# Group norm on one core: replacing a five-engine schedule by looped engine programs with GpSimd left idle

## The chip, the cores and the metric

The kernel runs on one core of a Trainium2 chip. The profile lists the core's work by engine: TensorE (PE; PEld is its weight load), VectorE (DVE), ScalarE (ACT), GpSimd (POOL) and SyncE (SP), which here only issues transfers. It counts 16 DMA engines, which in the kernel before read 134.22 MB from HBM and wrote 134.22 MB to it; SBUF is the memory on the chip that holds the tiles. The metric is device time in microseconds (us).

## The reference, cut to what matters

```python
B, C, H, W, G = 128, 1024, 32, 16, 32          # bfloat16
xr = x.reshape(B, G, C // G, H, W)
mu = xr.mean(axis=(2, 3, 4), keepdims=True)
var = ((xr - mu) ** 2).mean(axis=(2, 3, 4), keepdims=True)
xn = (xr - mu) / jnp.sqrt(var + 1e-5)
return xn.reshape(x.shape) * g[None, :, None, None] + b[None, :, None, None]
```

Each of the 4096 (image, group) pairs has 32 channels of 512 numbers. A tile is 128 pairs, one per partition, of 16,384 bf16 numbers: 4 MB. There are 32 tiles. Each must come in once (134 MB in all) and go out once (134 MB).

## The kernel before

Six tile buffers. Loads and stores share SyncE's queue. TensorE sums a tile (32 matmuls with an identity matrix, 512 columns each, into one 128x512 tile in PSUM, the memory that this kernel's matmuls write to), VectorE reduces the 512 sums to the mean, ScalarE squares and sums the tile in two halves and takes the square root, and three engines share the scaling of the 32 channels: 13 on GpSimd, 16 on VectorE, 3 on ScalarE.

```python
XBUFS = 6; UPFRONT = 6; RUN = 3; FIRST_RUN = 2; QUARTERS = 4
STORE_IN_PARTS = 2; ACT_SHARE = 2; LAST_SHARE = 3; POOL_SHARE = 13

def shifted(i):                      # these two tiles are loaded in quarters
    return i == 0 or i == NT - RUN

def A(i):                            # scale tile i
    if not in_parts(i):
        for n in range(POOL_SHARE):
            scale_on("pool", i, KC - LAST_SHARE - POOL_SHARE + n)
        for k in range(KC - LAST_SHARE - POOL_SHARE):
            scale_on("dve", i, k)
        ...
        return
    for c in range(NQ):              # the last two tiles: in quarters, stored as they are done
        for k in range(c * KQ, (c + 1) * KQ):
            on_act = i == NT - 1 and k >= (c + 1) * KQ - ACT_SHARE
            scale_on("act" if on_act else "dve", i, k)
        S(i, c, c + 1)

def finish(i):                       # called between ScalarE's two halves of tile i+1
    for k in range(KC - LAST_SHARE, KC):
        scale_on("act", i, k)
    S(i, 0, NQ)                      # store
    if i % RUN == FIRST_RUN - 1:     # after each third store: three loads
        ... L(j)
```

Everything is unrolled: 3885 instructions are recorded.

## Time and profile before

| | before |
|---|---|
| time, median of the first 3 runs (4 with the change beside it) | 632.48 us (632.44) |
| span of the profiled run | 630.9 us |
| busy: DMA / ACT / DVE / POOL / PE | 90% or more in 38 of 40 slices / 85% / 60% / 55% / 41% |
| DMA rate, 60 to 540 us | 429 to 434 GB/s |

First the page of the kernel before: span, busy time per engine, then rows of 40 slices of the span (a digit is the busy share in tenths), then the instruction fetches (queue, packets, MB, share), then three groups of instructions (line, engine, operation, output<-input, shapes, count; busy us, mean ns; idle time before them and what ended it).

```profile
span 630.9 us, 3885 instructions
PE 257.5 (41%) x1005; PEld 106.1 (17%) x1025; DVE 378.9 (60%) x645; ACT 537.6 (85%) x268; POOL 345.2 (55%) x523
...
DVE  0087766665665666277616774664766177777650
ACT  4599999998997699489949995996899499999950
POOL 0077776665664666177716664663776166777000
...
DMA  8999999999999999999999999999999999999996
...
q8 instruction: 8, 0.13, 0.1%
q14 instruction: 15, 0.12, 0.0%
...
L245 ACT ACTIVATE ja<-xt,negmean 128x8192 fp8e5<-128x8192 bf16 x60 | 426.5, 7109 | 51.5 <-DVE jd L190 51.4
...
L369 DVE TENSOR_SCALAR xt<-xt,scl,bia 128x512 bf16<-128x512 bf16 x536 | 351.3, 729 | 39.8 <-POOL bia L354 39.8
L369 POOL TENSOR_SCALAR xt<-xt,scl,bia 128x512 bf16<-128x512 bf16 x390 | 307.4, 801 | 3.4 <-POOL bia L354 0.3
```

Read it as follows. No compute engine fills its row; the DMA row is full from the second slice to the last but one. A scaling takes VectorE 729 ns while GpSimd also scales.

Next, stretches of the same kernel: busy us of each engine, granted clock, DMA share, GB/s.

```profile
300.00:360.00 60.00, 23.44 (x94) 9.76 (x96) 35.55 (x57) 51.45 (x25) 34.30 (x51) 0.70 1.00 432
...
600.00:620.00 20.00, 0.00 (x0) 0.00 (x0) 8.75 (x28) 8.73 (x11) 0.00 (x0) 0.50 0.98 415
620.00:631.00 11.00, 0.00 (x0) 0.00 (x0) 0.00 (x0) 0.00 (x0) 0.00 (x0) 0.50 0.53 226
```

In mid-run the DMA share is 1.00. At the end no engine computes; DMA alone runs, and more and more of its 16 engines fall idle (share 0.53 from 620 us on).

### The profile page before, as it was taken

The page shows a single profiled execution, that of the slowest core. Times are in us where ns is not written, and L with a number is a line of the kernel's source. Part 1 is how long each engine was busy: PE and PEld are TensorE (multiplying, and loading weights), DVE is VectorE, ACT ScalarE, POOL GpSimd, SP SyncE. Part 2 cuts the span into 40 slices and gives each one's busy share as a digit, 9 for nine tenths or more (in the row PEclk, how much of TensorE's full clock was granted, in tenths as well). Part 3 has the DMA queues.
Part 4 walks back from the last instruction along what each step waited for, and adds up shares of the span by engine and source line. Part 5 has one row for each costly group of instructions (what it writes and reads, how often), then busy time and mean ns, then how long its engine had stood idle before and what let it go on. Part 6 is the DMA issues. An engine that isn't in the chain of part 4 may idle for free.

```text
span 630.9 us, 3885 instructions
## 1 busy us (share of the span) xinstructions
PE 257.5 (41%) x1005; PEld 106.1 (17%) x1025; DVE 378.9 (60%) x645; ACT 537.6 (85%) x268; POOL 345.2 (55%) x523
## 2 busy tenths in 40 slices
PE   5567509009602750572086018404820770456000
PEld 2223203003201320230032003101300230112000
DVE  0087766665665666277616774664766177777650
ACT  4599999998997699489949995996899499999950
POOL 0077776665664666177716664663776166777000
PEclk9789858658855985587579559855965796679555
DMA  8999999999999999999999999999999999999996
GB/s 366 432 431 428 433 432 425 434 434 432 427 433 433 430 432 432 431 422 433 431 434 430 431 434 432 430 434 438 424 434 432 439 432 430 423 433 429 434 421 290
DMA packets 11063, 268.70 MB, mean 426 GB/s; under 512 B 1312, under 2 KB 1312, under 8 KB 1312
## 3 DMA queue, kind: packets, MB, share of 16 engines
q1 hardware_dynamic: 10944, 268.44, 99.1%
q8 instruction: 8, 0.13, 0.1%
q14 instruction: 15, 0.12, 0.0%
q10 hardware_dynamic: 96, 0.00, 0.0%
HBM read 134.22 MB, written 134.22 MB: 426 GB/s over the span
## 4 chain that ended last, share of the span: by engine, by line
DMA 66%; DVE 10%; ACT 9%; PE 8%; issue 3%; POOL 1%; SPq 1%; DVEq 0%; POOLq 0%; ACTq 0%
DMA out_dram<-xt 41%; DMA xt<-in_x_dram 25%; DVE xt L369 9%; PE pa L167 8%; ACT ja L245 8%; ACT xt L364 1%; SPq L105 0%; POOL scl L338 0%; POOL shift L344 0%; POOL bia L354 0%; ACT rstd L309 0%; DVE jd L190 0%; DVE rstd L313 0%; SPq L382 0%; DVEq L457 0%
## 5 line engine op out<-in xcount | busy, mean ns | idle before, releaser
L245 ACT ACTIVATE ja<-xt,negmean 128x8192 fp8e5<-128x8192 bf16 x60 | 426.5, 7109 | 51.5 <-DVE jd L190 51.4
L167 PE MATMUL pa<-xt,eye 128*128 128x512 bf16 x957 | 246.4, 418 | 320.1 <-DMA xt<-in_x_dram 317.5
L369 DVE TENSOR_SCALAR xt<-xt,scl,bia 128x512 bf16<-128x512 bf16 x536 | 351.3, 729 | 39.8 <-POOL bia L354 39.8
L369 POOL TENSOR_SCALAR xt<-xt,scl,bia 128x512 bf16<-128x512 bf16 x390 | 307.4, 801 | 3.4 <-POOL bia L354 0.3
L167 PEld LDWEIGHTS <-eye 128*128 128x128 bf16 x1024 | 106.0, 106 | 471.1 <-DMA xt<-in_x_dram 319.2
L338 POOL TENSOR_SCALAR scl<-gb,rstd 128x32 f32<-128x32 f32 x31 | 11.1, 359 | 216.2 <-DVE rstd L313 216.2
L190 DVE TENSOR_SCALAR_CACHE_REDUCE jd<-pa 128x512 bf16<-128x512 f32 x32 | 21.8, 682 | 103.0 <-PE pa L167 103.0
L364 ACT ACTIVATE xt<-xt,bia,scl 128x512 bf16<-128x512 bf16 x98 | 72.0, 799 | 0.8 <-DVE bia L325 0.8
L313 DVE RECIPROCAL rstd<-rstd 128x1 f32<-128x1 f32 x32 | 5.2, 163 | 83.8 <-ACT rstd L309 83.8
L245 ACT ACTIVATE ja<-xt,q 128x4096 fp8e5<-128x4096 bf16 x8 | 29.6, 3704 | 6.9 <-DVE jd L190 6.8
L344 POOL TENSOR_SCALAR shift<-scl,negmean 128x32 f32<-128x32 f32 x31 | 11.1, 357 | 3.1
L167 PE MATMUL pb<-xt,eye 128*128 128x512 bf16 x47 | 11.4, 389 | 0.5 <-DMA xt<-in_x_dram 0.4
L245 ACT ACTIVATION_READ_ACCUMULATOR ja<-xt,negmean 128x1 f32 x60 | 11.2, 187 | 0.0
L309 ACT ACTIVATE rstd<-s,v 128x1 f32<-128x1 f32 x30 | 8.8, 294 | 2.8
L274 POOL TENSOR_SCALAR v<-s 128x1 f32<-128x1 f32 x30 | 5.9, 197 | 8.2 <-ACT ja L245 5.8
L217 POOL TENSOR_SCALAR off<-negmean,q 128x1 f32<-128x1 f32 x2 | 0.6, 308 | 16.0 <-DVE jd L190 16.0
L354 POOL TENSOR_TENSOR bia<-shift,gb 128x32 f32<-128x32 f32 x31 | 7.8, 251 | 2.6
L309 ACT ACTIVATE rstd<-var,eps_t 128x1 f32<-128x1 f32 x2 | 0.6, 296 | 8.3 <-DVE jv L293 8.3
L160 DVE COPY gb<-gb_p 128x64 f32<-128x64 f32 x1 | 0.2, 224 | 5.2 <-PE gb_p L152 5.2
L120 ACT ACT_TABLE_LOAD x1 | 1.3, 1283 | 1.7 <-PEq L446 1.7
L190 DVE DVE_READ_ACCUMULATOR jd<-pa 128x1 f32 x32 | 2.5, 79 | 0.0
L245 ACT ACTIVATION_READ_ACCUMULATOR ja<-xt,q 128x1 f32 x8 | 1.5, 186 | 0.0
(18 smaller groups left out, 5.0 us busy)
## 6 DMA issues: line engine op xcount, KB each, us to landing
xt<-in_x_dram SPq DMA_DIRECT2D x30, 4096.0 KB, 29.0
out_dram<-xt SPq DMA_DIRECT2D x30, 4096.0 KB, 36.8
xt<-in_x_dram SPq DMA_DIRECT2D x8, 1024.0 KB, 16.5
out_dram<-xt SPq DMA_DIRECT2D x8, 1024.0 KB, 19.0
gb_b<-in_g_dram ACTq DMA_DIRECT2D x1, 2.0 KB, 3.2
gb_b<-in_b_dram ACTq DMA_DIRECT2D x1, 2.0 KB, 5.3
```

What stands on the lines that cost most here:

```text
L120: chain("act", nc.scalar.activation(out=warm[:], in_=eps_t[:], func=ACT.Sqrt))
L167: nc.tensor.matmul(out=ps[:], lhsT=eye[:], rhs=st["xt"][:, k * MMN : (k + 1) * MMN], start=(k == lo), stop=(k == hi - 1),),
L190: nc.vector.tensor_scalar(out=jd[:], in0=ps[:], scalar1=-inv_n, scalar2=seed, op0=ALU.mult, op1=ALU.add, accum_out=total[:],),
L245: nc.scalar.activation(out=ja[:, 0:w], in_=st["xt"][:, k * w : (k + 1) * w], func=ACT.Square, bias=bias, scale=scale, accum_out=sq, satura ...
L274: nc.gpsimd.tensor_scalar(out=v0[:], in0=s0[:], scalar1=inv_n, scalar2=EPS, op0=ALU.mult, op1=ALU.add,),
L309: nc.scalar.activation(out=rstd[:], in_=last_sum[:], func=ACT.Sqrt, bias=bias[:], scale=scale),
L313: chain("dve", nc.vector.reciprocal(out=rstd[:], in_=rstd[:]))
L338: nc.gpsimd.tensor_scalar(out=scl[:], in0=gam, scalar1=rstd[:], scalar2=None, op0=ALU.mult),
L344: nc.gpsimd.tensor_scalar(out=shift[:], in0=scl[:], scalar1=st["negmean"][:], scalar2=None, op0=ALU.mult,),
L354: nc.gpsimd.tensor_tensor(out=bia[:], in0=shift[:], in1=bet, op=ALU.add),
L364: inst = nc.scalar.activation(out=span, in_=span, func=ACT.Identity, bias=bia, scale=scl)
L369: inst = eng.tensor_scalar(out=span, in0=span, scalar1=scl, scalar2=bia, op0=ALU.mult, op1=ALU.add,)
```

## The change

Intent: give each engine its own program with fixed addresses, looped over the six ring slots, so that few instructions are needed; take GpSimd out; let TensorE sum 12 of the 32 chunks of 512 columns while VectorE adds the other 20 in pairs in one instruction; move the mean to ScalarE. Loads and stores keep their order, but no tile is split any more. The diff cut to its core:

```diff
-    for i in range(NT):
-        Q(i)                       # squares on ScalarE (and the previous tile's last 3 scalings)
-        if i + 1 < NT:
-            M(i + 1); R0(i + 1)    # 32 chunks on TensorE, mean on VectorE
-        V(i); A(i)                 # scale/bias on GpSimd, scaling on GpSimd and VectorE
+    def in_rounds(e, one):         # on TensorE, ScalarE, VectorE, each for itself
+        with nc.Fori(0, TRIPS, 1, engines=[e.engine]) as t:       # TRIPS = 5
+            for c in range(SLOTS):                                # SLOTS = 6
+                one(c, t + 1)
+        for c in range(NT - LOOPED):                              # the last two tiles
+            one(c, TRIPS + 1)
```
```diff
+    # VectorE
+    def one(c, turn):
+        follows = not isinstance(turn, int)
+        then = (c + 1) % SLOTS, turn + (c + 1) // SLOTS
+        if follows:
+            pair(*then)            # the next tile's 20 chunks: 5,120 + 5,120 elements, summed
+        e.wait_ge(stded[c], turn)
+        ...                        # reciprocal, scl, bia: 32 elements each
+        for k in range(KC):        # all 32 scalings of this tile
+            ...
+        ts.then_inc(done[c], 1)
```

(Cut: ScalarE's mean from PSUM, its two squares and two small activations; TensorE's 12 matmuls per tile, 32 for the last; SyncE's list of loads and stores; allocations and semaphores.)

## The prediction

Two passages are cut below, and marked, because no trace or run had shown them: a ceiling for the DMA rate (the trace's stretches show 429 to 434 GB/s), and the item on loop turns, a guess. ("Its packet records" are those of the trace of the kernel before.) The sum came to 632.3 us. It is not written out; what stands of it is the kernel before (632.44 us), 0.7 off for the quarters, 0 to 2 on for the tail, and under 1 either way for fetches. The term for loop turns was put behind the DMA limit and shows, as far as can be read, only in "12 to 15 us per loop turn": 6 x (19.4 - 17) and 6 x (19.4 - 16.5) are 14.4 and 17.4, 2.4 more each.

Four of its numbers do not name all they come from, but the trace of the kernel before gives it. Pairing: a 128x512 sum takes VectorE 0.682 us and a 128x1 reciprocal 0.163; with that as the fixed part, 10 x (0.682 - 0.163) + 0.163 = 5.4. ScalarE's mean: three 128x512 scalings in a row take 2.11 us, 0.70 each, and reading a sum 0.19, together 0.9. Fetches: 8 of 16 KB at 1.01 us and 15 of 8 KB at 0.31 make 13 us. Issue to data: the first load was issued at 0.79 us, its first packet started at 1.82.

> **What bounds the kernel now.** The DMA engines. The row of slices shows DMA busy 90% or more in 38 of 40 slices; stretches of 60 us show a share of 1.00 to 1.01 and 429 to 434 GB/s from 60 to 540 us. ACT is busy 85%, DVE 60%, POOL 55%, PE 41%. The DMA-issuing queue waits long (362 us for VectorE's scaling, 211 for stores), but transfers are always outstanding, so that costs nothing. [...] Its packet records: a 32 KB row takes 1.213 us, an 8 KB piece 0.309. 64 tile transfers are 8 rows each per DMA engine: 64 x 8 x 1.213 = 621 us. The span is 630.9: about 2 us of start, 3 of late packets, and a tail in which the 16 engines finish between 624 and 629.5. Only these 10 us can be won.
>
> **What the change does.**
> - Bytes stay. Tiles 0 and 29 are no longer loaded, 30 and 31 no longer stored, in quarters: 4 x 8 x (4 x 0.309 - 1.213) = -0.7 us per DMA engine.
> - Instruction fetch (0.25 MB, 13 us of one DMA engine, 0.8 if spread) may shrink or be repeated each turn: under 1 us.
> - VectorE: with GpSimd idle, a 128x512 scaling keeps the pace of the trace's last tiles (13 in 4.29 us: 0.33 us), not 0.73. Per tile 32 x 0.33 = 10.5; pairing 5,120 elements, an estimate, 5.4 (from 0.68 for 512, fixed part taken off); small ones with waits 0.9: 17 us.
> - ScalarE: two squares 14.5, mean about 0.9, two small ones 0.6, waits 0.4: 16.5 us; it scales no more.
> - TensorE: 12 x 0.42 = 5 us instead of 13.
> - [...]
>
> A tile in and out costs DMA 19.4 us, so 17 and 16.5 leave over 2 us each: 12 to 15 us per loop turn. Nearly all of the compute change is off the critical path.
>
> **The tail.** Today the last load lands at 571 us; six stores of 9.7 us follow. In the new kernel ScalarE starts tile 29 at about 557 and ends tile 31 near 606, VectorE scales it by 618, and only then its whole store is issued; the slowest DMA engine needs it at about 619, and data starts about 1 us after issue. So the quarters' 0.7 us is about given back: 0 to 2 us lost here.
>
> **Predicted: 632.3 us, range 630.2 to 636.0.** Faster by over 2%: 0.01; within 2%: 0.95; slower by over 2%: 0.04.
>
> **What would show it.** DMA share 1.00 from 60 to 600 us; row packets of 1.213 us; DVE busy near 530 us, scaling at 0.33 to 0.41 us each; ACT near 510; POOL near 0; the last store issued near 618; the chain of waits mostly DMA, ending in one 9.7 us store.
>
> **What would make it wrong.** A VectorE period above 19.4 us (pairing far slower, or many us per branch) would pace the whole loop: several per cent slower. A pace of 15 to 16 us would remove the tail loss: 630.5. Pairing the next tile before scaling this one ties a store to the next load; if that empties the DMA queue at a change of phase, slices under 90% would show it.

## The result, and the profile after

| | before | after |
|---|---|---|
| median (4 runs each) | 632.44 us | 633.04 us |
| lowest to highest | 632.23 to 633.02 | 632.46 to 633.53 |
| ratio of fast runs | | 1.0008 (95%: 0.999 to 1.0025) |

A ratio is the mean time of one kernel's fast runs over that of the other's of the same rounds, so it is not quite the ratio of the medians. The two kernels are the same within 2%, and no difference is resolved. Almost everything inside changed. The same lines of the page, after:

```profile
span 630.3 us, 2508 instructions
PE 157.6 (25%) x405; PEld 52.0 (8%) x405; DVE 522.3 (83%) x1185; ACT 504.0 (80%) x258; POOL 0.8 (0%) x6
...
DVE  1579999999996998599589949994997799499671
ACT  0799999999996999399859958993999399769930
POOL 0000000000000000000000000000000000000000
...
DMA  8999999999999999999999999999999999999996
...
q8 instruction: 1, 0.02, 0.0%
q14 instruction: 3, 0.02, 0.0%
...
L203 ACT ACTIVATE ja<-ring,nm 128x8192 fp8e5<-128x8192 bf16 x64 | 455.9, 7123 | 2.1
L268 DVE TENSOR_SCALAR ring<-ring,scl,bia 128x512 bf16<-128x512 bf16 x1024 | 333.7, 408 | 1.2
...
L236 DVE SCALAR_TENSOR_TENSOR jp<-ring 128x5120 fp8e5<-128x5120 bf16 x31 | 170.1, 5488 | 63.8 <-DMA ring<-in_x_dram 63.8
```

VectorE scales nearly twice as many spans (1024 instead of 536) in less busy time (333.7 instead of 351.3 us), because one takes 408 ns instead of 729. Pairing adds 170 us to it. The DMA row is the same, digit for digit. Instruction fetches fell from 23 packets to 4.

The same stretches, after:

```profile
300.00:360.00 60.00, 13.95 (x36) 4.60 (x36) 51.23 (x117) 48.93 (x25) 0.00 (x0) 0.59 1.01 434
...
600.00:620.00 20.00, 0.00 (x0) 0.00 (x0) 11.69 (x37) 5.04 (x4) 0.00 (x0) 0.50 0.89 383
```

In mid-run DMA moves what it moved before. In the tail its share falls from 0.98 to 0.89: there is a hole. Here is VectorE's order of time after the change, where it is not waiting for a load (start, us, engine, line, operation, count):

```profile
264.36 0.20 DVE L253 RECIPROCAL rstd<-std 128x1 f32<-128x1 f32 x1
...
265.16 10.43 DVE L268 TENSOR_SCALAR ring<-ring,scl,bia 128x512 bf16<-128x512 bf16 x32
275.50 5.49 DVE L236 SCALAR_TENSOR_TENSOR jp<-ring 128x5120 fp8e5<-128x5120 bf16 x1
280.91 0.15 DVE L236 DVE_READ_ACCUMULATOR jp<-ring 128x1 f32 x1
280.91 0.21 DVE L253 RECIPROCAL rstd<-std 128x1 f32<-128x1 f32 x1
```

From one reciprocal to the next are 280.91 - 264.36 = 16.55 us: VectorE's period per tile. Loading and storing a tile costs every DMA engine 16 rows of 32 KB at 1.213 us each, 19.4 us. So VectorE has 2.9 us of slack per tile, or about 17 us per loop turn of six, as long as it waits for nothing else.

### Who ends the program

The traces record 16 landings (semaphore increments) for every transfer: 1,248 for the 78 transfers before, 1,056 for the 66 after. That is as many as the page counts DMA engines, and they are read here as one per DMA engine. The last two stores, for tiles 30 and 31, are informative. All tables of landings below are from those records, in us:

```
                     store 30 lands on       last store    last landing   last landing minus
                   fastest median slowest      issued                    slowest of store 30
before              614.3   616.0   620.1      611.8 *        629.9            9.8
after               613.9   614.2   619.4      616.4          629.1            9.7
                                               (* last quarter of it)
```

A whole store takes one DMA engine 8 x 1.213 = 9.7 us. In both kernels the program ends 9.7 us after the slowest DMA engine finished store 30. After the change, eleven of the sixteen are done by 614.8 and idle until store 31 is issued: that is the hole. But the slowest works until 619.4, when store 31 has already been issued (its first packets start at 617.2). This gives a theory and its rivals:

- **Theory A.** The slowest of the 16 DMA engines ends the program, before and after. Compute is off its path, except where the last store is issued later than that engine needs it. The hole costs nothing.
- **Rival B.** The hole, 2.5 us per DMA engine on average from 612 to 618 us, is lost time: the change gained that much and gave it back in the tail.
- **Rival C.** VectorE's added work, or the loops, cost time that cancels a gain elsewhere.

### The profile page after: what moved, and what is told of

Its sections match the earlier page's. It is cut to its first block, busy times and chain, and to the rows that moved or that the text cites. A ratio compares the mean times of both kernels' runs of the same rounds, so it can differ in the third digit from the quotient of the medians.

```text
span 630.3 us, 2508 instructions
## 1 busy us (share of the span) xinstructions
PE 157.6 (25%) x405; PEld 52.0 (8%) x405; DVE 522.3 (83%) x1185; ACT 504.0 (80%) x258; POOL 0.8 (0%) x6
## 4 chain that ended last, share of the span: by engine, by line
DMA 63%; DVE 26%; ACT 7%; issue 0%; SPq 0%; DVEq 0%
DMA out_dram<-ring 43%; DMA ring<-in_x_dram 20%; DVE ring L268 16%; DVE jp L236 9%; ACT ja L203 7%; DVE bia L259 0%; DVE scl L255 0%; ACT jm L195 0%; SPq L123 0%; ACT var L213 0%; DVE rstd L253 0%; ACT std L217 0%; DVEq L275 0%; SPq L309 0%; SPq L278 0%
## 5 line engine op out<-in xcount | busy, mean ns | idle before, releaser
L203 ACT ACTIVATE ja<-ring,nm 128x8192 fp8e5<-128x8192 bf16 x64 | 455.9, 7123 | 2.1
L268 DVE TENSOR_SCALAR ring<-ring,scl,bia 128x512 bf16<-128x512 bf16 x1024 | 333.7, 408 | 1.2
L173 PE MATMUL ps<-ring,eye 128*128 128x512 bf16 x404 | 157.4, 571 | 411.8 <-DMA ring<-in_x_dram 411.8
L236 DVE SCALAR_TENSOR_TENSOR jp<-ring 128x5120 fp8e5<-128x5120 bf16 x31 | 170.1, 5488 | 63.8 <-DMA ring<-in_x_dram 63.8
L195 ACT ACTIVATE jm<-ps 128x513 fp8e5<-128x513 f32 (+1 forms) x32 | 19.2, 601 | 95.0 <-DVE jp L236 95.0
L173 PEld LDWEIGHTS ps<-ring,eye 128*128 128x128 bf16 x404 | 51.9, 134 | 516.9 <-issue 467.2
L203 ACT ACTIVATION_READ_ACCUMULATOR ja<-ring,nm 128x1 f32 x64 | 12.0, 187 | 0.0
L217 ACT ACTIVATE std<-sq,var 128x1 f32<-128x1 f32 x32 | 9.4, 295 | 1.0
L213 ACT ACTIVATE var<-sq,eps_t 128x1 f32<-128x1 f32 x32 | 9.4, 295 | 1.0
L259 DVE SCALAR_TENSOR_TENSOR bia<-scl,nm,gb 128x32 f32<-128x32 f32 x32 | 8.0, 251 | 1.1
```

The costliest lines, as they stand in the source:

```text
L173: mm = e.matmul(out=sums(c), lhsT=eye[:], rhs=slot(c)[:, k * MM_FREE : (k + 1) * MM_FREE], start=(k == 0), stop=(k == chunks - 1),)
L195: e.activation(out=jm[:, 0 : src.shape[1]], in_=src, func=ACT.Identity, scale=-inv_n, accum_out=nm[:, c : c + 1], saturate=False,).then_in ...
L203: e.activation(out=ja[:], in_=slot(c)[:, h * (F // 2) : (h + 1) * (F // 2)], func=ACT.Square, bias=nm[:, c : c + 1], scale=1.0, accum_out= ...
L213: e.activation(out=var[:], in_=sq[:, 0:1], func=ACT.Identity, bias=eps_t[:], scale=inv_n).then_inc(varred[c], 1)
L217: e.activation(out=std[:, c : c + 1], in_=sq[:, 1:2], func=ACT.Sqrt, bias=var[:], scale=inv_n).then_inc(stded[c], 1)
L236: e.scalar_tensor_tensor(out=jp[:], in0=slot(c)[:, first : first + w], scalar=1.0, in1=slot(c)[:, first + w : first + 2 * w], op0=ALU.mult ...
```

## The experiments

Twelve kernels ran, each beside the kernel before on the same chip. Except for the two with half the stores, all results were correct. The new kernel's ratio to compare with is 1.0008. It was not run again beside them: they ran on three chips, on which the kernel before had medians of 632.83, 632.76 and 632.62 us, against 632.44 beside the new kernel. A ratio is known to about 0.0015, so the difference of two ratios to about 0.002, or 1.4 us: where a run is said below to lie less than that above or below the new kernel, the times alone do not show it, and the traces have to.

### 1. Closing the hole

```diff
-            e.wait_ge(done[i % SLOTS], i // SLOTS + 1)
-            e.dma_start(out=o_v[i], in_=slot(i))...
+            parts = 4 if i == NT - 1 else 1
+            for q in range(parts):
+                e.wait_ge(done[i % SLOTS], i // SLOTS + 1 + q)
+                e.dma_start(<quarter q of tile i>)...
```

> The new kernel with its last tile stored in four parts, each as soon as its eight scalings are done (first part issued near 608.6 us instead of 616.4). Theory A, the slowest of the 16 DMA engines ends the program and was not waiting in the tail (its share of store 30 landed at 619.4 us, data for store 31 flowed from 617.2): the hole of 613 to 617 us in the DMA row closes, but the time stays, within 0.7 us of the new kernel: 0.999 to 1.002 of before. Rival B, the hole of 2.5 us per engine is lost time: 2 to 2.5 us faster than the new kernel, 0.997 of before or less.

Measured: 633.53 us, ratio 1.0011 (0.9997 to 1.0024). DMA's row of 40 slices between 600 and 632 us, first of the new kernel, then of this one:

```profile
DMA  9899899899899799431219299199199191000000
```

```profile
DMA  9979899799799499498997998999954211000000
```

The hole in the first row ("431219", about 612 to 617 us) is gone in the second, where the DMA engines run out one after the other ("954211"). The last landing is at 630.4 us instead of 629.1. That is lag from before the edit matters: store 26 already landed on the slowest DMA engine at 581.9 us instead of 580.7, and store 29 at 610.9 instead of 609.7. From there to the end are two stores in both, 19.5 and 19.4 us. So the hole was free. Rival B falls.

### 2. Making the hole deeper

```diff
+            if is_last(c, turn):
+                for _ in range(2):
+                    waste(1850)          # a useless VectorE instruction of about 2 us, and a drain
             for k in range(KC):          # the last tile's scaling
```

> The new kernel with about 4.2 us of useless VectorE work before the last tile's scaling, so the last store is issued near 620.6 us. Theory A (slowest DMA engine, free at 619.4 us in the new kernel): it waits about 2 us, time up 1.5 to 2.7 us, about 1.004 of before. Rival B (all of the hole counts): up 4.2 us, 1.007 to 1.008.

Measured: 635.35 us, ratio 1.0035 (1.0021 to 1.0049), 2.3 us above the new kernel's median, not the 4.2 of rival B. The last store was issued at 621.6 us, 5.2 us later than in the new kernel's profile (this run was 0.9 us behind already at 569); store 30 landed on the slowest DMA engine at 620.5. So it waited about 2 us: issue plus the 0.85 us to the first packet gives 622.5.

### 3. Taking the pairing out

```diff
-PE_CHUNKS = 12
+PE_CHUNKS = 32                         # and no pair() on VectorE
```

> The new kernel without pairing: TensorE sums all 32 chunks of every tile, VectorE loses 170 us of work. Theory A (compute off the path except in the tail): DMA share 1.00 until 600 us as before; tile 29's mean comes about 4 us later (32 chunks in 9.4 us against pairing in 5.5), ScalarE paces the last three tiles, last store near 620.5 us, time up 1.5 to 4 us: 1.003 to 1.007 of before. Rival C (VectorE's load costs time): faster than the new kernel by over 2 us.

Measured: 633.96 us, ratio 1.002 (1.0005 to 1.0035), about 0.9 us above the new kernel: below the 1.5 to 4 us expected of A, not resolved from it, and no gain, as C would have it. The last store was issued at 619.2 us, 2.8 us later than in the new kernel, not 4; with 0.85 us to the first packet that is just when the slowest DMA engine became free (620.2). VectorE lost 170 us of work, and the time did not fall. What pairing buys is not throughput: it shortens the chain from the landing of tile 29 to the last store: ScalarE starts the squares of tile 29 at 557.71 us with pairing and at 561.35 without.

### 4. How much VectorE work is free

```diff
             ts.then_inc(done[c], 1)
+            if follows and c < 4:
+                waste(1800)              # about 2 us; the second run: twice waste(2560), about 6 us
```

> The new kernel with about 2 us of useless VectorE work after four of the six tiles of each loop turn: 8 us a turn, 40 us in all. Theory A (VectorE has about 17 us of slack per turn: 6 x (19.43 - 16.55)): VectorE busy rises by about 38 us, the time stays within 0.7 us of the new kernel (0.999 to 1.003 of before). Rival C (VectorE's work is paid): up to 40 us slower, 1.06.

> The same with about 24 us a turn, more than the slack of 17. Theory A: VectorE now paces from the first turn on; first scaling at 35.7 us, 31 tiles of 16.55, 5 turns of 24, one scaling and one store: 675 to 695 us. If the slack were larger than 24 us a turn: 633.

Measured: with 8 us a turn 634.58 us, ratio 1.0028 (1.0012 to 1.0045). VectorE's busy time rose by 40 us (562.4 instead of 522.3), the time by about 1.5 us: within the ratio expected of A, but not within 0.7 us of the new kernel. The profile shows where: DMA was idle for about 1.5 us between 117 and 123 us (two slices of 2.5 us busy to 6 and 5 tenths only), in the first loop turn, when compute has not yet gathered a lead. Up to 200 us there is no other such gap, and store 30 landed at 617.7 us in the median instead of 614.2. With 24 us a turn 687.95 us (one run, state unknown), inside the predicted 675 to 695. Stretches of this run:

```profile
300.00:360.00 60.00, 15.58 (x39) 5.23 (x41) 59.38 (x116) 44.18 (x21) 0.00 (x0) 0.59 1.00 430
500.00:560.00 60.00, 12.91 (x35) 4.48 (x36) 59.53 (x124) 51.66 (x25) 0.00 (x0) 0.59 0.94 394
```

VectorE is now busy over 59 of 60 us and sets the pace; the DMA share is still 1.00 at 300 us and 0.94 at 500. The slack of about 17 us a turn is bracketed by this, not measured: 8 us nearly fit, 24 do not. Over the whole program less was free: VectorE's busy time rose by 112 us (634.7 instead of 522.3) and the time by 55, so about 57 us were absorbed, 11 a turn (an estimate from these two runs).

### 5. Is an idle GpSimd the reason for the fast scaling?

```diff
     # GpSimd, after its two small constants
+        with nc.Fori(0, 32, 1, engines=[e.engine]) as t:
+            for n in range(16):
+                e.tensor_scalar(out=junk[:], in0=junk[:], ...)   # 128x320 bf16, its own buffer
+                e.drain()
```

> The new kernel with GpSimd kept busy for its first part by 512 useless operations on a small SBUF buffer of its own. Theory A (an idle GpSimd is what gives VectorE its 0.33 us per scaling): while GpSimd works, scalings take 0.55 to 0.75 us each, the DMA share falls under 0.9 in these slices, time 660 to 760 us. Rival E (the loop, fixed addresses or the order made scaling faster): scaling stays at 0.41 us, 633 us.

Measured: 722.97 us (one run, state unknown), inside the 660 to 760. GpSimd worked until about 410 us. Lines of this run: groups from 100 to 400 us, then from 460 to 700 us.

```profile
L157 POOL TENSOR_SCALAR junk<-junk 128x320 bf16<-128x320 bf16 x376 | 236.0, 628 | 64.8 <-issue 64.8
L278 DVE TENSOR_SCALAR ring<-ring,scl,bia 128x512 bf16<-128x512 bf16 x376 | 224.1, 672 | 0.4
```

```profile
L278 DVE TENSOR_SCALAR ring<-ring,scl,bia 128x512 bf16<-128x512 bf16 x430 | 140.2, 409 | 0.5
L246 DVE SCALAR_TENSOR_TENSOR jp<-ring 128x5120 fp8e5<-128x5120 bf16 x12 | 65.8, 5487 | 15.8 <-DMA ring<-in_x_dram 15.8
```

Then three lines from the same run in order of time (start, us):

```profile
308.71 0.46 POOL L157 TENSOR_SCALAR junk<-junk 128x320 bf16<-128x320 bf16 x1 [0.15 <-issue]
309.23 5.47 DVE L246 SCALAR_TENSOR_TENSOR jp<-ring 128x5120 fp8e5<-128x5120 bf16 x1
309.32 5.70 POOL L157 TENSOR_SCALAR junk<-junk 128x320 bf16<-128x320 bf16 x1 [0.15 <-issue]
```

In one and the same run, a scaling takes 672 ns beside a working GpSimd and 409 without, and the DMA share is 0.73 from 280 to 340 us. From 100 to 400 us there are as many GpSimd operations as scalings, 376 of each. The three lines show a long GpSimd operation too: the one that starts 0.09 us into a pairing takes 5.70 us instead of 0.46, and ends 0.32 us after the pairing. The pairing itself hardly changed (5.47 and 5.49 us). What lengthens them was not shown. So idling GpSimd is what makes room for pairing and 32 scalings on VectorE: with it busy, VectorE cannot keep the DMA pace.

### 6. GpSimd's share moved to VectorE in the old kernel

```diff
-POOL_SHARE = 13
+POOL_SHARE = 0
```

> The kernel before with GpSimd's 13 scalings per tile given to VectorE (29 on VectorE, 3 on ScalarE), nothing else. Theory A: scaling falls from 0.73 to about 0.41 us in the records, VectorE needs 9.6 us per tile instead of 11, the time stays within 0.3% of before. Rival F (GpSimd's help was needed in the old structure): slower by over 0.5%.

Measured: 635.06 us, ratio 1.0039 (1.0023 to 1.0056). The scaling did fall to 407 ns, VectorE's busy time from 378.9 to 329.9 us, yet the time rose by 2.3 us: more than A expected and less than F, and F's reason does not hold, since VectorE had become quicker. The landings say what happened: store 30 landed on the slowest DMA engine at 622.6 us instead of 620.1, while the median stayed at 616.1. One DMA engine had fallen behind, in a DMA row as full as before. The next experiments find why.

### 7. Unrolling

All three loops unrolled, then only VectorE's:

```diff
-        with nc.Fori(0, TRIPS, 1, engines=[e.engine]) as t:
+        for t in range(TRIPS):
             for c in range(SLOTS):
                 one(c, t + 1)
```

> The new kernel with its three loops unrolled, same order, same waits on constants. Theory A: loop turns lie in the slack; time within 0.3% of the new kernel (0.998 to 1.004 of before), instruction fetches rise from under 10 to near 20 and DMA time of others than the main queue from 0.4 to about 0.8 us per engine. Rival D (a loop turn costs over 1 us that is paid): 5 us or more faster, 0.993 of before.

> The new kernel with only VectorE's loop unrolled; TensorE and ScalarE stay looped. Theory H (VectorE's instruction fetches all fall on one DMA engine, 0.6 to 1.0 us each, and the slowest DMA engine ends the program): like the fully unrolled one, 2 to 3.5 us above the new kernel, 1.004 to 1.007 of before, the slowest DMA engine 8 to 9 us behind the fast ones in its landings before the last store, its lag growing in steps at the fetches. Rival I (the other engines' loops made the difference): within 1 us of the new kernel.

Measured: 636.05 us, ratio 1.0053 (1.004 to 1.0067), and 635.88 us, ratio 1.0049 (1.0035 to 1.0062). The first missed what I had expected of A (within 0.3% of the new kernel) and went against D: loops do not cost time, they save almost 3 us. Its 14 fetches were also fewer than the near 20 expected. The second hit theory H, formed after the first. The fetch lines of the kernel with only VectorE unrolled:

```profile
q14 instruction: 10, 0.08, 0.0%
q8 instruction: 1, 0.02, 0.0%
```

Against the new kernel there are seven more 8 KB fetches, of 0.31 us each by their packet records: 2.2 us of one DMA engine in all, 0.14 us if spread over 16. But the lag of the last DMA engine to land (behind the mean of the six first) grows at just those moments:

```
VectorE unrolled: fetch at         160.2  229.0  291.5  363.8  425.1  505.7  566.4 us
lag of the slowest after it          3.9    4.7    5.5    6.1    6.9    8.1    9.3 us
step in that one transfer            1.0    0.8    0.8    0.6    0.6    1.0    1.1 us
new kernel (no fetch from 108 to 576 us): lag 2.8 us at 111 us, 5.4 us before the last store
```

The records do not name the DMA engine. That it is the same one each time is read from the lag, which keeps what it gains but for dips of 0.2 to 0.5 us. The packets, strung end to start, agree: they put all seven fetches on one chain of the sixteen, the one that has moved the fewest bytes at each of them (in 26 of its 434 steps a second packet would fit as well). They also show where the step comes from: the row packet that follows the fetch on that chain takes 1.61 to 1.88 us instead of 1.213, so fetch and delay together are 0.70 to 0.98 us. The whole set of landings, with 9.7 us to compare with in the last column:

```
                           store 30 lands on     last store   last     last minus   fetch packets
                         median     slowest       issued     landing    slowest        (in span)
after                     614.2      619.4        616.4       629.1       9.7              4
VectorE late (2)          614.5      620.5        621.6       632.7      12.2              4
no pairing (3)            614.5      620.2        619.2       630.2      10.0              5
all unrolled (7)          614.4      622.8        619.1       632.5       9.7             14
VectorE unrolled (7)      614.6      623.3        619.3       632.9       9.6             11
before                    616.0      620.1        611.8 *     629.9       9.8             23
before, no POOL_SHARE (6) 616.1      622.6        614.7 *     632.3       9.7             22
bursts of four (9)        614.8      620.2        617.0       629.9       9.7              4
VectorE +8 a turn (4)     617.7      621.8        618.2       631.4       9.6              5
VectorE +24 a turn (4)    669.2      670.5        673.9       685.0      14.5              5
GpSimd busy (5)           708.5      710.3        706.7       719.9       9.6              4
(* last quarter; experiment 1 is left out: its four parts share one semaphore and cannot be told apart)
```

In every run but number 2 and the one with 24 us a turn, where the store really came late, the program ends one store after the slowest DMA engine (in number 3 the store was late by about 0.3 us: all sixteen landed within 0.1 us of each other). In the runs without added work in the loop the median says nothing about it: it moves from 614.2 to 616.1 us, and not with the end. The old kernel has the most fetches (23) but not the most lag (620.1 us): its recorded instructions are divided over TensorE (1,005 matmuls), VectorE (645) and GpSimd (523). Where VectorE's grew to 1,035 (experiment 6, 622.6 us) or to 1,185 unrolled (7, 622.8 and 623.3 us), one DMA engine fell behind. That the instructions of each engine might be fetched by a DMA engine of their own is a guess: it fits these landings, but only VectorE's seven fetches were placed on one chain, and for the other engines it was not shown. Why the packet after a fetch takes longer stays open.

### 8. Taking the DMA limit away

Both kernels storing only half of each tile's columns, a wrong result:

```diff
-            e.dma_start(out=o_v[i], in_=slot(i))...
+            e.dma_start(out=o_v[i][:, 0 : F // 2], in_=slot(i)[:, 0 : F // 2])...
```

> Wrong result on purpose: the new kernel storing only the first half of each tile's columns, so a tile costs DMA 14.55 us instead of 19.4. Theory A: now VectorE paces at 16.55 us per tile: first scaling at 35.7, 31 tiles, last scaling 10.5, half a store and the end 7 to 8 us: 562 to 575 us. If DMA were not what binds the full kernel, the time would stay near 633.

> Wrong result on purpose: the kernel before storing only half of each tile. Theory A: ScalarE paces at 16.71 us per tile (read from its square roots at 65.84, 82.56 and 99.27 us): 32.4 + 31 x 16.71 + about 10: 558 to 570 us, within 2% of the other half-store run. Rival G (the change did shorten the compute and DMA hides it): this one is 3% or more slower than the other half-store run.

Measured: 567.21 us for the new kernel, ratio 0.8965, and 563.07 us for the old, ratio 0.8901, both to the whole old kernel. First a stretch of the new one, then of the old one:

```profile
220.00:280.00 60.00, 16.57 (x40) 5.53 (x42) 59.68 (x137) 57.44 (x27) 0.00 (x0) 0.59 0.94 390
```

```profile
220.00:280.00 60.00, 24.72 (x94) 10.10 (x96) 45.48 (x73) 59.72 (x30) 42.86 (x63) 0.73 0.92 384
```

Columns after the window are PE, PEld, DVE, ACT and POOL. Freed of a quarter of the DMA work, the new kernel is held by VectorE (59.68 of 60 us) at 16.55 us per tile, the old by ScalarE (59.72 of 60) at 16.71. So DMA does bind the full kernels, and behind it the change did not shorten the compute: it moved the second limit from ScalarE to VectorE at nearly the same pace. The old kernel is even 4 us quicker here, probably because its last tile is scaled by two engines and stored in quarters; that was not tested.

### 9. A try at something better

Loads in seven bursts instead of nine, since the new kernel's records show packets of up to 2.2 us (2.19 at 59.7 us, 2.15 at 390.5), instead of 1.213, where DMA changes from loading to storing:

```diff
-            if i % RUN == FIRST_RUN - 1:
-                for j in range(max(SLOTS, i + 1 + SLOTS - RUN), min(i + 1 + SLOTS, NT)):
+            if i in (2, 6, 10, 14, 18, 22, 25):
+                for j in range(loaded, i + 1 + SLOTS):
                     load(j)
```

> A try for a better one: the new kernel with loads in seven bursts (3, four each, then 3) instead of nine, so DMA changes between loading and storing less often. The slowest DMA engine gains about 0.3 us of lag at each such change: 0.5 to 1 us less lag before the last store (5.4 us in the new kernel), time 0 to 1 us below the new kernel: 0.998 to 1.001 of before. If the longer bursts leave VectorE or the DMA queue waiting: slower by over 1 us.

Measured: 632.95 us, ratio 1.0005 (0.9992 to 1.0019). The time cannot be told from the new kernel's. The lag of the slowest DMA engine before the last store did not shrink: 5.4 us behind the median, against 5.2 in the new kernel. No version that clearly beats either kernel was found.

## Why the prediction was right, and where its steps were off

The prediction was 632.3 us with a range of 630.2 to 636.0, "within 2%" at 0.95; measured were 633.04 us and a ratio of 1.0008. What the runs test is that DMA binds and compute lies off its path. That the number came within 0.8 us is partly luck: its small terms below, of 0.3 to 2 us, were off in both directions and are near or below what these runs resolve.

- *DMA binds, compute is off the path.* Right. The DMA share in 60 to 580 us is 1.00 to 1.01; the row packets have a median of 1.213 us in both traces; half the stores make both kernels over 10% faster (experiment 8); 40 us of useless VectorE work cost about 1.5 us, and 112 us made it 55 us slower (4).
- *VectorE 17 us per tile, scaling 0.33 us, pairing 5.4 us.* Right: 16.55, 10.43 / 32 = 0.326, and 5.49. Its busy time was to be near 530 us and is 522. ScalarE, predicted at 510, is 504.
- *Quarters: -0.7 us per DMA engine.* The mean busy time of the main queue per DMA engine fell by 1.2 us, from 625.4 to 624.2: in the kernel before the 8 KB pieces averaged 0.314 us and the rows 1.218, where the prediction took the medians. Direction right, size too small. The slowest landing of store 30 came earlier too (620.1 to 619.4), but that cannot be put down to it: experiment 1, the same kernel up to its last store, had 1.2 us more lag at store 26.
- *The tail: last store issued near 618, needed at 619, 0 to 2 us lost.* Issued at 616.4, needed at 619.4, nothing lost (experiments 1 and 2). That the slowest DMA engine counts, not the average, was the right step, and it is what kept the hole from mattering.
- *Instruction fetch: "under 1 us", "0.8 if spread".* This step was wrong as a way to cost it. In the new structure fetches of VectorE's instructions are not spread: unrolled they cost almost 3 us (635.88 against 633.04, experiment 7). The looped program keeps all fetches to four packets and so avoids a loss that the same program unrolled had. Against the old kernel no gain was measured (ratio 1.0008); that its instructions were divided over three engines may be why, but that was not shown.
- *Loop turns*. Too pessimistic: no fetch comes with a turn (none from 108 to 576 us in the new kernel), and with half the stores (8), where VectorE sets the pace, one reciprocal follows the other after 16.54 to 16.56 us from tile 1 to tile 29, loop turns included. The unrolled version is not faster (636.05 us).
- What the prediction did not have: outside the span the new kernel takes about 0.3 us more (1.9 to 2.2 us between time and span, 1.7 to 1.8 before). The new kernel's trace has two 8 KB fetches that start after the end of its span (631.4 and 632.2 us), that of the kernel before none; whether they are the cause was not tested.

So the answer to where a gain could have come from and did not is this: the busy time taken away (100 us on TensorE, 34 on ScalarE, 344 on GpSimd) lay behind the DMA limit, and VectorE, with 143 us more, came as close to that limit as ScalarE had been.

## What to carry to other kernels

When the DMA row is full, cost a change on the slowest DMA engine, not on the mean of the sixteen: look at the spread of the last landings (store 30's here: 5.8 us before, 5.5 after), and ask which few packets one engine carries alone. Freed engine time gained nothing here (170 us of VectorE work taken out: ratio 1.002 instead of 1.0008, experiment 3), nor did storing the last tile earlier (1.0011, experiment 1). So measure the slack (by adding useless work, or by storing less) before working on it. If a long unrolled stream sits on one engine beside a full DMA row, try looping it: here VectorE's program took 633.04 us looped and 635.88 unrolled.
